# Cosine on one core: whole turns taken off in one VectorE operation, the angle counted in turns

## The chip, the core and the metric

One core of one Trainium2 chip runs the whole program. The metric is the time of one execution on the device in microseconds (us); lower is better. The engines are named as in the profile: PE (TensorE), DVE (VectorE), ACT (ScalarE), POOL (GpSimd), SP (SyncE, which here issues most DMAs).

## What is computed

Attention with pooled queries, then a mixture of experts with eight experts of 288 tokens each, then a dense layer pair with a cosine between its halves. The change touches the last function alone:

```python
def _moe_ref(x, w_gate, w1, w2):            # x: 2304 x 512, 8 experts, 288 tokens each
    ...
    for e in range(E):
        mask = assigned == e
        h = np.maximum(x[mask] @ w1[e], 0.0)
        out[mask] = h @ w2[e]

def _moe2_ref(x, w_in, w_out):              # 2304 x 512, 512 x 2048, 2048 x 512
    h = x @ w_in
    g = h * np.cos(h)
    return g @ w_out
```

The inputs are 64-bit or 32-bit floats of which the kernel makes a high and a low float16 half each; a product of two such matrices is three float16 matmuls (high with high, high with low, low with high).

## The kernel before, in words

**Stages.** The attention takes the first 450 us or so of the span. Then comes `moe`: the tokens are routed to the eight experts one expert after the other (`route`), and each expert's rows run through three passes in the order of the table `PLAN`: `ffn1(i)` for expert i (two matmuls with a ReLU between them, L1353 and L1367), `ffn2_in(j)` for block j of 256 tokens (the product with `w_in`, L1429, and the cosine), and `ffn2_out(j)` (the product with `w_out`, L1454). From expert 2 on, PLAN is `ffn1(j)`, `ffn2_in(j)`, `ffn2_out(j)` for j = 2, 3, ... , and block 8 comes last without an `ffn1`.

**The cosine.** `ffn2_in(j)` fills eight banks of PSUM per block, one for each pair of feature tiles: 24 matmuls of 256 columns a bank (2 tiles, 4 slices of the contraction, 3 products). For each bank `cosine` runs a chain over 128x512 elements. `u` is the bank (the trace calls it `h`), scaled by the constant `U_UP`. ACT writes the number of whole turns as an integer (L1396, T for short below). DVE takes `turns` times 2 pi off in two steps, with the high part of 2 pi (L1398) and with its low part (L1400). ACT takes the sine of half the angle (L1402) and squares it (L1404). DVE forms the product with `u` (L1407), which frees the bank. ACT rounds it to float16 (L1412, `gh`), and POOL subtracts that from it (L1414, `gl`). L1398 and L1407 read one operand from PSUM and one from SBUF; L1400 reads both from SBUF. The tile `turns` has four buffers (`TB`), `r1` has three, and there are four banks.

**Who else is at work then.** The search of `route` is a chain of rounds (8 for an expert): DVE compares (L999, `ge`), PE counts (L965 for the first three experts, L976 and L985 for the later ones, with a copy L981 or, on ACT, L979 between the two), DVE compares with the room left (L1009, `hit`), PE sums (L1012), and DVE makes the next candidates (L1014 `near`, L1023, L1027 `cand`). Weights of the next expert land by DMA (L1249 and L1251, on SP's queue), ACT rounds them (L1278) and DVE makes the low halves (L1282). Up to about 590 us the 64-bit `w_out` is decoded as well (`split64`: L228, L241 to L256, on SP, DVE, ACT and POOL). The tokens of the next expert are gathered by POOL (L1205) and transposed by DMA (L1214, SP).

**What sets the order.** Each engine runs its instructions in the order in which they were written, and a class `Order` decides that order while the program is built: each task says with `yield ENGINE, size` what it wants next, and `Order.go` gives each engine to the request that could start first by a table of costs (`COST`: a fixed part, a part per element and a latency, for DVE 0.07 us, 0.00105 us and 0.15 us). A request that is taken away or made shorter therefore moves the instructions of all engines from there on. An engine does not pass over an instruction that waits.

Of the kernel before, what the change touches and what calls it, by code (L numbers as in the profile page):

```python
# [13 lines left out]
AF = mybir.ActivationFunctionType  # L14
OP = mybir.AluOpType
# [28 lines left out]
PE, ACT, DVE, POOL, SP = "PE", "ACT", "DVE", "POOL", "SP"  # L44
# [23 lines left out]
U_UP = Y_UP * WIN_UP  # L68
O_EVAC = -2.0 / (U_UP * WOUT_UP)
TWO_PI = 2.0 * math.pi  # L70
PI_HI = round(TWO_PI * 512.0) / 512.0
PI_LO = TWO_PI - PI_HI

class Order:
# [31 lines left out]
    def start(self, task, rank, at=None):  # L108
        t = self.now
        if at is not None:  # L110
            self.now = at
        self.resume(task, rank)
        self.now = t

    def mark(self, *key, at=None):

        t = self.now
        self.done[key] = t if at is None else at
        for since, rank, task in self.parked.pop(key, []):
            self.now = max(self.done[key], since)  # L120
            self.resume(task, rank)
        self.now = t
# [795 lines left out]
def moe(od, tc, logits, x_dram, list_dram, before, same, ones, fixed, wih, wil, todo, w1, w2, w_out, out):  # L918
    nc = tc.nc
    V = nc.vector  # L920
    with ExitStack() as ctx:
# [375 lines left out]
        def y_tile(j):  # L1297
            if j not in yT:
                yT[j] = tuple(ac.tile([128, KD, NB], F16, name=n, bufs=3) for n in ("yh", "yl"))
            return yT[j]  # L1300
# [10 lines left out]
        def bank():  # L1311

            b = next(banks)
            if b >= 4:
                yield "read", b - 4
            return b, ps.tile([128, 512], F32, name="h", bufs=4)
# [56 lines left out]
        def g_tiles():  # L1373
            return [ac.tile([128, NF2, NB], F16, name=n) for n in ("gh", "gl")]
# [3 lines left out]
        def ffn2_in(j):  # L1378
            yh, yl = y_tile(j)
            gh, gl = halves[j] = g_tiles()  # L1380
            who = range(j * NB // CAP, ((j + 1) * NB - 1) // CAP + 1)
            for i in who:
                yield "listed", i
            nc.sync.dma_start(rows_sb[:, 2 * j:2 * j + 2], list_dram[j * NB:(j + 1) * NB, 0].rearrange("(c p) -> p c", p=128))

            def cosine(u, f, b):

                n = NF2 // 2 * j + f // 2
                if n >= TB:
                    yield "cosine", n - TB  # L1390
                if n >= TB - 1:
                    yield "product", n - TB + 1
                yield ACT, 512
                turns = ac.tile([128, 512], I32, name="turns", bufs=TB)
                r = ac.tile([128, 512], F32, name="r1", bufs=TB - 1)
                nc.scalar.activation(turns, u, AF.Copy, scale=1.0 / (TWO_PI * U_UP))  # L1396
                yield DVE, 512
                V.scalar_tensor_tensor(r, turns, -PI_HI * U_UP, u, op0=OP.mult, op1=OP.add)  # L1398
                yield DVE, 512
                V.scalar_tensor_tensor(r, turns, -PI_LO * U_UP, r, op0=OP.mult, op1=OP.add)  # L1400
                yield ACT, 512
                nc.scalar.activation(r, r, AF.Sin, scale=0.5 / U_UP)  # L1402
                yield ACT, 512
                nc.scalar.activation(r, r, AF.Square)  # L1404
                yield DVE, 512
                g = turns.bitcast(F32)
                V.scalar_tensor_tensor(g, r, 0.5, u, op0=OP.subtract, op1=OP.mult)  # L1407
                mark("read", b)
                mark("product", n)
                yield ACT, 512  # L1410
                g = g.rearrange("p (e n) -> p e n", e=2)
                nc.scalar.activation(gh[:, f:f + 2], g, AF.Copy)  # L1412
                yield POOL, 512
                nc.gpsimd.tensor_tensor(gl[:, f:f + 2], g, gh[:, f:f + 2], op=OP.subtract)  # L1414
                mark("g", j, f)
                mark("cosine", n)


            for f in range(0, NF2, 2):
                b, u = yield from bank()  # L1420
                for e in range(2):
                    fs = slice((f + e) * 128, (f + e + 1) * 128)
                    for kk in range(KD):
                        for i in who:
                            yield "y", i, kk
                        yield "win", kk * (F2 // NW) + (f + e) * 128 // NW
                        yield PE, 3 * NB
                        for z, (x, y) in enumerate(((wih, yh), (wih, yl), (wil, yh))):
                            nc.tensor.matmul(u[:, e * NB:(e + 1) * NB], x[:, kk, fs], y[:, kk],  # L1429
                                             start=kk == 0 and z == 0, stop=kk == KD - 1 and z == 2)  # L1430
                start(cosine(u, f, b), 1)
# [64 lines left out]
```

## Time and profile before

| what | us |
| --- | --- |
| median of 3 runs | 1140.61 |
| lowest and highest | 1136.2 and 1143.11 |
| the profiled execution, its own time | 1142.8 |
| its span in the profile | 1140.8 |
| PE busy in the span | 1033.8 (91%) |
| DVE, ACT, POOL busy | 825.4, 706.0, 575.3 |

The span runs from the first to the last recorded instruction; 2.0 us of the profiled execution lie around it. "Busy" is the union of an engine's instructions. A matmul's end is modelled and lies behind the start of the next one, so that a busy PE can still be waited on for a little. In brackets behind an instruction of the timeline stand the idle time in front of it and the instruction that ended it. The granted clock is TensorE's, as a share of full speed (2.4 GHz), so that 0.50 is the lower of its two levels, 1.2 GHz.

### The profile page before, as it was taken

Reading aid. Unit: us, or ns where it says so; the run is one execution under the profiler, and the core shown is the slowest. Engines: PE = TensorE matmul, PEld = TensorE weight load, DVE = VectorE, ACT = ScalarE, POOL = GpSimd, SP = SyncE. Lnnn points to the kernel's source line nnn. Section 1 sums busy time; section 2 is a strip of 40 time slices with the busy share of each in tenths; the row PEclk is TensorE's granted clock in tenths of the full one; section 3 lists DMA queues with packets and bytes.
Section 4 is the critical chain, followed back from the end, with each engine's and each line's share of the span. In section 5 each row is a group of like instructions: output and inputs, shape, how many; then the busy total and the mean of one; then the engine's idle time right before and its main releaser. Section 6 shows DMA issues by size and latency. Waiting matters only on the chain. (4 is left out here: it accounts for less than half of the span.)

```text
span 1140.8 us, 25414 instructions
## 1 busy us (share of the span) xinstructions
PE 1033.8 (91%) x10020; PEld 714.7 (63%) x10020; DVE 825.4 (72%) x1816; ACT 706.0 (62%) x1314; POOL 575.3 (50%) x591
## 2 busy tenths in 40 slices
PE   4898999989998998339889999999999999999997
PEld 2465666656665666227755758577585775858673
DVE  7988988889988887688987818749387482732642
ACT  3888989899998996346863526437154362632542
POOL 4789989888999897442651221313203132130312
PEclk7999999999999999559989999999999999999999
DMA  8987878867765641475616213231331350300000
GB/s 206 233 169 157 178 164 171 171 159 169 158 143 135 132 96 39 143 161 164 183 63 175 84 40 96 76 100 35 114 96 57 106 143 19 95 10 10 4 17 18
DMA packets 187383, 128.00 MB, mean 112 GB/s; under 512 B 138944, under 2 KB 157376, under 8 KB 187264
## 3 DMA queue, kind: packets, MB, share of 16 engines
q1 hardware_dynamic: 184000, 116.36, 42.7%
q0 software_dynamic: 2976, 9.44, 2.5%
q8 instruction: 78, 1.28, 0.5%
q10 hardware_dynamic: 288, 0.59, 0.2%
q14 instruction: 41, 0.34, 0.1%
HBM read 83.40 MB, written 9.45 MB: 81 GB/s over the span
## 5 line engine op out<-in xcount | busy, mean ns | idle before, releaser
L673 POOL TENSOR_TENSOR pl<-p,ph 128x512 f16<-128x512 f32 x192 | 239.2, 1260 | 31.8 <-ACT ph L668 24.4
L1414 POOL TENSOR_TENSOR gl<-turns,gh 128x512 f16<-128x512 f32 x72 | 96.0, 1338 | 282.5 <-ACT gh L1412 281.8
L568 DVE TENSOR_REDUCE nm<-s 128x1 f32<-128x512 f32 x288 | 185.1, 678 | 13.8 <-PE s L526 13.0
L1429 PE MATMUL h<-yl,wih 128*128 128x256 f16 x576 | 157.7, 274 | 2.5 <-DVE yl L1339 2.5
L1429 PE MATMUL h<-yh,wih 128*128 128x256 f16 x576 | 157.8, 274 | 1.8 <-DVE turns L1407 1.8
L1429 PE MATMUL h<-yh,wil 128*128 128x256 f16 x576 | 157.7, 274 | 0.0
L687 PE MATMUL t<-q,k 128*128 128x512 f16 (+1 forms) x576 | 136.0, 291 | 11.0 <-ACT p L664 7.0
L526 PE MATMUL s<-k,q 128*128 128x512 f16 (+3 forms) x480 | 126.3, 341 | 21.2 <-DVE nm L568 15.2
L688 PE MATMUL t<-q,k 96*128 96x512 f16 (+1 forms) x576 | 136.5, 291 | 0.6 <-DMA q<-q 0.6
L664 ACT ACTIVATE p<-t 128x512 f32<-128x512 f32 (+1 forms) x208 | 115.0, 581 | 18.8 <-PE t L688 14.0
L708 PE MATMUL acc<-vv,ph 128*128 128x130 f16 (+1 forms) x1124 | 119.2, 222 | 0.0
L1429 PEld LDWEIGHTS <-wih 128*128 128x128 f16 x1152 | 108.4, 98 | 17.1 <-DVE turns L1407 2.3
L708 PE MATMUL acc<-vv,pl 128*128 128x65 f16 (+1 forms) x1124 | 112.6, 192 | 0.0
L1454 PE MATMUL o<-woh,gl 128*128 128x512 f16 x288 | 109.2, 379 | 2.7 <-POOL gl L1414 2.6
L708 PEld LDWEIGHTS <-ph 128*128 128x128 f16 (+1 forms) x1152 | 101.8, 106 | 15.2 <-issue 7.5
L668 ACT ACTIVATE ph<-p 128x512 f16<-128x512 f32 x180 | 111.1, 642 | 0.4
L1327 DVE SCALAR_TENSOR_TENSOR hl<-h,hh 128x288 f16<-128x288 f32 x64 | 29.1, 455 | 111.4 <-ACT hh L1325 95.1
L1454 PE MATMUL o<-woh,gh 128*128 128x512 f16 x288 | 109.1, 379 | 0.0
L1454 PE MATMUL o<-wol,gh 128*128 128x512 f16 x288 | 109.1, 379 | 0.0
L708 PEld LDWEIGHTS <-pl 128*128 128x128 f16 (+1 forms) x1152 | 93.7, 102 | 11.4 <-POOL pl L673 1.0
L1353 PE MATMUL h<-xx,w1h 128*128 128x288 f16 x512 | 99.9, 296 | 0.0
L1454 PEld LDWEIGHTS <-gh 128*128 128x128 f16 x576 | 53.3, 98 | 59.5 <-issue 2.5
(226 smaller groups left out, 2469.5 us busy)
## 6 DMA issues: line engine op xcount, KB each, us to landing
wraw<-in_moe_w_dram SPq DMA_DIRECT2D x64, 512.0 KB, 4.7
vr<-in_v_dram SPq DMA_DIRECT2D x32, 288.0 KB, 3.7
kr<-in_k_dram SPq DMA_DIRECT2D x30, 288.0 KB, 3.3
qr<-in_q_dram SPq DMA_DIRECT2D x32, 256.0 KB, 3.1
raw<-in_moe_w_in_dram SPq DMA_DIRECT2D x16, 512.0 KB, 5.1
raw<-in_moe_w_out_dram SPq DMA_DIRECT2D x16, 512.0 KB, 4.0
k<-k SPq DMA_DIRECT2D x32, 144.0 KB, 3.6
x_dram<-xs SPq DMA_DIRECT2D x16, 160.0 KB, 2.5
```

Of the source, the lines that this page charges most:

```text
L526: T.matmul(to[lo:hi], ops["q", u][0][:, c, lo:hi], ops["k", u, i][0][:, keys, :].rearrange("p a b -> p (a b)"), start=True, stop=True)
L568: V.tensor_reduce(st["nm", u][:, c, g:g + 1], s, AX.X, OP.max)
L664: A.activation(f[:, :w], s[:, :w], AF.Exp, scale=QK_DOWN)
L668: A.activation(ph[:, b], f[:, :w], AF.Copy)
L673: G.tensor_tensor(pl[:, b], f[:, :w], ph[:, b], op=OP.subtract)
L687: T.matmul(s[:, to:to + w], k1[:, j], q1[:, cols], start=True, stop=False)
L688: T.matmul(s[:, to:to + w], k2[0:96, j], q2[0:96, cols], start=False, stop=True)
L708: T.matmul(acc[lo:hi, to + a:to + 2 * (D + 1)], t[z][:, at:at + hi - lo], vv[:, j, a:], start=j == first and z == 0 and to == 0, stop=j == ...
L1353: nc.tensor.matmul(ph[:, :CAP].rearrange("p (j t) -> p j t", j=3), x[:, kk, fs], y[:, :, kk], start=kk == 0 and z == 0, stop=kk == KD - 1 ...
L1414: nc.gpsimd.tensor_tensor(gl[:, f:f + 2], g, gh[:, f:f + 2], op=OP.subtract)
L1429: nc.tensor.matmul(u[:, e * NB:(e + 1) * NB], x[:, kk, fs], y[:, kk], start=kk == 0 and z == 0, stop=kk == KD - 1 and z == 2)
L1454: nc.tensor.matmul(po, x[:, f, cs], y[:, f], start=f == 0 and z == 0, stop=f == NF2 - 1 and z == 2)
```

## The change

DVE's two operations on `turns` become one. It multiplies `u` by the same factor with which ACT counted the turns, and subtracts the integer from it: what is left is the angle in turns, between -0.5 and 0.5, and the sine takes it times pi. The new operation reads its first operand from PSUM and its second (integers) from SBUF. The constants of 2 pi's two parts go.

```diff
-PI_HI = round(TWO_PI * 512.0) / 512.0
-PI_LO = TWO_PI - PI_HI
...
                 nc.scalar.activation(turns, u, AF.Copy, scale=1.0 / (TWO_PI * U_UP))
                 yield DVE, 512
-                V.scalar_tensor_tensor(r, turns, -PI_HI * U_UP, u, op0=OP.mult, op1=OP.add)
-                yield DVE, 512
-                V.scalar_tensor_tensor(r, turns, -PI_LO * U_UP, r, op0=OP.mult, op1=OP.add)
+                V.scalar_tensor_tensor(r, u, 1.0 / (TWO_PI * U_UP), turns, op0=OP.mult, op1=OP.subtract)
                 yield ACT, 512
-                nc.scalar.activation(r, r, AF.Sin, scale=0.5 / U_UP)
+                nc.scalar.activation(r, r, AF.Sin, scale=math.pi)
```

Lines of the changed kernel behind the cosine have numbers lower by 3 than before (L1407 is L1404 there), lines of `moe` ahead of it by 2 (L999 is L997, L1282 is L1280), and the new operation is L1397.

One request for DVE fewer per bank moves the order of every engine from the first cosine on; nothing stands differently ahead of it. On DVE in `ffn2_in(0)`, in the later rounds of a search, there stood before (`mag` is a step of decoding `w_out`, `w1l` and `w2l` are low halves of expert weights, `r` the cosine's angle, a number behind a name tells buffers apart):

```order
L999 TENSOR_TENSOR ge<-near,cand 128x270
L1398 SCALAR_TENSOR_TENSOR r_10185<-turns,h 128x512
L241 SCALAR_TENSOR_TENSOR mag<-raw_10017,near 128x512
L1009 TENSOR_SCALAR hit_10229<-r,room 8x15
L1400 SCALAR_TENSOR_TENSOR r_10185<-turns,r_10185 128x512
L1014 SCALAR_TENSOR_TENSOR near<-r,wbit 128x15
L1407 SCALAR_TENSOR_TENSOR turns<-r_10127,h 128x512
L1023 TENSOR_REDUCE near<-near 128x1
L1282 SCALAR_TENSOR_TENSOR w1l<-wraw,w1h 128x512
L1027 TENSOR_TENSOR cand<-near,kbit 128x15
L1282 SCALAR_TENSOR_TENSOR w2l<-wraw,w2h 128x512
L999 TENSOR_TENSOR ge<-near,cand 128x270
```

Now a round that belongs to the same pass reads:

```order
L250 TENSOR_TENSOR low<-low,sg 128x512
L1404 SCALAR_TENSOR_TENSOR turns<-r_10072,h 128x512
L1007 TENSOR_SCALAR hit_10159<-r,room 8x15
L1397 SCALAR_TENSOR_TENSOR r_10124<-h,turns 128x512
L1012 SCALAR_TENSOR_TENSOR near<-r,wbit 128x15
L1021 TENSOR_REDUCE near<-near 128x1
L1025 TENSOR_TENSOR cand<-near,kbit 128x15
L997 TENSOR_TENSOR ge<-near,cand 128x270
```

Of six operations of 512 elements in a round three are left here. The first four rounds of that pass hold as many as before, because weights and decoding (`w1l`, `w2l`, `mag`, `low`, `wol`) have moved up into them.

On DVE in `ffn2_in(2)`, a round of a later search, before:

```order
L1009 TENSOR_SCALAR hit_12135<-r,room 128x15
L1398 SCALAR_TENSOR_TENSOR r_12125<-turns,h 128x512
L1014 SCALAR_TENSOR_TENSOR near<-r,wbit 128x15
L1400 SCALAR_TENSOR_TENSOR r_12125<-turns,r_12125 128x512
L1023 TENSOR_REDUCE near<-near 128x1
L1407 SCALAR_TENSOR_TENSOR turns<-r_12074,h 128x512
L1027 TENSOR_TENSOR cand<-near,kbit 128x15
L999 TENSOR_TENSOR ge<-near,cand 128x270
L1398 SCALAR_TENSOR_TENSOR r_12168<-turns,h 128x512
L981 CAST part<-r 90x48
```

And a round now:

```order
L1007 TENSOR_SCALAR hit_12087<-r,room 128x15
L1404 SCALAR_TENSOR_TENSOR turns<-r_12030,h 128x512
L1012 SCALAR_TENSOR_TENSOR near<-r,wbit 128x15
L1021 TENSOR_REDUCE near<-near 128x1
L1025 TENSOR_TENSOR cand<-near,kbit 128x15
L997 TENSOR_TENSOR ge<-near,cand 128x270
L1404 SCALAR_TENSOR_TENSOR turns<-r_12062,h 128x512
L979 CAST part<-r 90x48
```

From `hit` to the next `part` four operations of 512 elements have become two. On PE the last two counts of such a search now stand 15 matmuls behind the sum before them, all within `ffn2_in`, where before 24 and 15 lay between, the latter within `ffn2_out`.

## Rows read from the trace of the kernel before

**Rows 1.** The page's head and its part 1: busy time of each engine.

```profile
span 1140.8 us, 25414 instructions
...
PE 1033.8 (91%) x10020; PEld 714.7 (63%) x10020; DVE 825.4 (72%) x1816; ACT 706.0 (62%) x1314; POOL 575.3 (50%) x591
```

**Rows 2.** Stretches of 10 us: length, PE, PEld, DVE, ACT, POOL busy (instructions), clock, DMA, GB/s.

```profile
560.00:570.00 10.00, 10.00 (x116) 8.13 (x113) 10.00 (x23) 9.27 (x18) 8.06 (x6) 1.00 0.65 166
570.00:580.00 10.00, 5.87 (x66) 4.05 (x65) 10.00 (x22) 9.54 (x17) 9.68 (x7) 0.77 0.32 92
580.00:590.00 10.00, 10.00 (x73) 6.52 (x72) 7.90 (x19) 6.62 (x12) 6.49 (x5) 0.72 0.04 16
...
720.00:730.00 10.00, 8.36 (x60) 4.30 (x61) 8.36 (x20) 6.00 (x11) 4.24 (x4) 1.00 0.00 0
...
1050.00:1060.00 10.00, 10.00 (x94) 8.96 (x92) 5.68 (x9) 6.17 (x12) 1.16 (x1) 1.00 0.01 2
```

**Rows 3.** Timeline of PE: start, duration, instruction, idle before it and its releaser.

```profile
573.73 0.60 PE L965 MATMUL r<-ge,own 128*8 128x15 f16 x18 [0.95 <-DVE ge L999]
...
579.14 0.60 PE L965 MATMUL r<-ge,own 128*8 128x15 f16 x18 [1.85 <-DVE ge L999]
...
720.54 0.31 PE L976 MATMUL r<-own,ge 128*90 128x48 f16 x3 [0.72 <-DVE ge L999]
...
723.50 0.17 PE L1012 MATMUL r<-hit,ones 128*128 128x15 f16 x1 [0.54 <-DVE hit L1009]
...
727.44 0.31 PE L976 MATMUL r<-own,ge 128*90 128x48 f16 x3 [0.52 <-DVE ge L999]
...
927.29 0.28 PE L1429 MATMUL h<-yh,wih 128*128 128x256 f16 x1 [1.81 <-DVE turns L1407]
...
948.30 0.39 PE L1454 MATMUL o<-woh,gl 128*128 128x512 f16 x1 [0.48 <-POOL gl L1414]
...
1078.17 0.39 PE L1454 MATMUL o<-woh,gl 128*128 128x512 f16 x1 [0.59 <-POOL gl L1414]
...
1080.13 0.39 PE L1454 MATMUL o<-woh,gl 128*128 128x512 f16 x1 [0.48 <-POOL gl L1414]
```

**Rows 4.** One line's instructions: duration in ns (least/median/most), first and last start.

```profile
L1400 DVE SCALAR_TENSOR_TENSOR r<-turns,r x72: 665/815/2419, 550.9 to 1117.2; 128x512 f32<-128x512 int32 x72
...
L1398 DVE SCALAR_TENSOR_TENSOR r<-turns,h x72: 665/680/689, 549.2 to 1116.5; 128x512 f32<-128x512 int32 x72
...
L1327 DVE SCALAR_TENSOR_TENSOR hl<-h,hh x64: 434/457/458, 513.9 to 1037.1; 128x288 f16<-128x288 f32 x64
```

**Rows 5.** Groups by line from 600 us on: count, busy us, mean ns, idle before.

```profile
L1400 DVE SCALAR_TENSOR_TENSOR r<-turns,r 128x512 f32<-128x512 int32 x64 | 70.7, 1104 | 0.8
```

**Rows 6.** Timeline of DVE in `ffn2_in(7)`.

```profile
1052.49 0.69 DVE L1400 SCALAR_TENSOR_TENSOR r<-turns,r 128x512 f32<-128x512 int32 x1
...
1054.99 0.68 DVE L1407 SCALAR_TENSOR_TENSOR turns<-r,h 128x512 f32<-128x512 f32 x1
1055.59 0.68 DVE L1400 SCALAR_TENSOR_TENSOR r<-turns,r 128x512 f32<-128x512 int32 x1
...
1065.20 0.68 DVE L1407 SCALAR_TENSOR_TENSOR turns<-r,h 128x512 f32<-128x512 f32 x1
...
1067.18 1.54 DVE L1400 SCALAR_TENSOR_TENSOR r<-turns,r 128x512 f32<-128x512 int32 x1
1068.65 0.68 DVE L1407 SCALAR_TENSOR_TENSOR turns<-r,h 128x512 f32<-128x512 f32 x1
```

**Rows 7.** Timeline of ACT in `ffn2_in(7)`.

```profile
1053.21 0.63 ACT L1402 ACTIVATE r<-r 128x512 f32<-128x512 f32 x1 [1.48 <-DVE r L1400]
...
1054.25 0.62 ACT L1404 ACTIVATE r<-r 128x512 f32<-128x512 f32 x1
```

**Rows 8.** Timeline of POOL in `ffn2_in(7)`.

```profile
1067.02 1.16 POOL L1414 TENSOR_TENSOR gl<-turns,gh 128x512 f16<-128x512 f32 x1 [2.29 <-ACT gh L1412]
```

**Rows 9.** Timeline of ACT at the start of `ffn2_in(5)`.

```profile
923.06 1.06 ACT L1278 ACTIVATE w2h<-wraw 128x1024 f16<-128x1024 f32 x1 [4.30 <-DMA wraw<-in_moe_w_dram]
```

## Prediction

> **What bounds the kernel now.** I read the page's head first: PE is busy 91% of the span [rows 1], so it is the engine that sets the end, and what DVE saves counts only where PE waits for it. The stretches of 10 us then show how little that is: in most of the second half PE is busy 10.00 of 10.00, as at 1050 us. The holes are at 570 to 590 us, with PE at 5.87 of 10 and the granted clock at 0.77 and 0.72, and at 720 us with 8.36 [rows 2]; the stretches at 790 and 860 us look like that at 720. So I went to PE's timeline and looked at who ends each idle time: behind 550 us it is nearly always DVE or the cosine's chain [rows 3]. Last I asked why DVE is late. The removed operation has a median of 815 ns and reaches 2419, while L1398, which does the same arithmetic with one operand in PSUM, never leaves 665 to 689 ns [rows 4]. The timeline shows why: an L1400 of 1.54 us begins at 1067.18 while POOL's `gl` runs from 1067.02 to 1068.18, and goes through only behind it [rows 6, 8]. Both of L1400's operands lie in SBUF.
>
> **The change part by part.** *What goes from DVE.* 72 operations; 64 of them took 70.7 us, 1104 ns each [rows 5], so about 79 us of DVE in all. What stays is one operation with a PSUM operand, 680 ns like L1398 [rows 4]. ACT, POOL and PE keep all their work. None of the 79 us is on the path as such, for PE covers it; what is on the path are PE's waits, which I take one by one. A matmul of 256 columns is shown with 0.28 us [rows 3] though 94 of them fit into 10 us [rows 2], 0.106 us each, so an idle time in front of one means some 0.17 us more of lost pace. I add that to each wait (for the 512-column matmul as an estimate by the same difference).
>
> *The cosine alone, blocks 7 and 8.* Here DVE has nothing else. From one L1407 to the next it takes 1068.65 - 1065.20 = 3.45 us [rows 6], while PE fills a bank in 24 x 0.106 = 2.55. Five of the eight banks run at that pace, and `ffn2_out` waits twice for `gl`, 0.59 and 0.48 [rows 3], 1.4 us with the pace; block 8 shows the same pair. Without L1400 the cycle in the new order is: DVE's angle to the sine 0.72 (1052.49 to 1053.21), the sine 0.63, the square to the product 0.74 (1054.25 to 1054.99), the product to DVE's next operation 0.60 (1054.99 to 1055.59) [rows 6, 7], 2.69 us in all. Five banks at 0.76 less are 3.8 us, more than the 1.4 waited for. Both blocks: 2.8 us. Bounds 0 and 2.8; the upper one, because nothing else is late next.
>
> *Block 5.* `ffn2_in(5)` waits 1.81 us for a bank [rows 3], 2.0 with the pace. Its cause is a weight for which ACT waits 4.30 us [rows 9], and that stays. Behind it the chain to the first L1407 loses one DVE operation (0.6) and, in the new order, the `turns` of the next bank that stood ahead of the sine on ACT (0.5): 1.1 us, bounds 0 and 2.0. Its `gl` wait of 0.48 [rows 3], 0.65 with the pace, goes as in block 7.
>
> *Blocks 2 to 4, the search.* PE waits 0.72, 0.54 and 0.52 us for `ge` and `hit` at the end of `ffn2_in(2)` [rows 3], 2.3 us with the pace; blocks 3 and 4 repeat it, 6.8 us together. These rounds are queued on DVE behind L1400s that POOL holds. Four large operations between two counts become two, but the order now also puts the last counts only 15 matmuls (1.6 us) behind the sum before them, and a part of the copies sits on ACT. I keep 0.9 us of wait per block and take 4.1; bounds 0 and 6.8.
>
> *Block 0, 560 to 590 us.* DVE is busy 10.00 of 10.00 twice over, and PE waits 0.95 and 1.85 us for `ge` [rows 2, 3] and twice more, shorter, for `hit`. PE's idle time from 570 to 580 is 4.1 us. Then the granted clock falls to 0.77 and 0.72: a mean of full and half rate, so 4.6 and 5.6 us at 1.2 GHz, which cost about 1.4 (PE was busy 0.59 of it) and 2.8 us. Together 8.3 us, the upper bound. The lower is 0, for ACT is busy 9.27 and 9.54 there [rows 2], and DVE stands in line for its squares. In the new order the first four rounds keep their six large operations, since decoding and weights move up; the last three, where PE waited, have about three. I take half, 4.1 us.
>
> *Sum.* 2.8 + 1.1 + 0.65 + 4.1 + 4.1 = 12.75 us, from 1142.8 (the profiled execution) to 1130.0. That execution lies 2.2 us above the median of the runs, so for a median I say 1128.
>
> One rule is weighed here. The rows say that operations with an operand in PSUM are not held by POOL, but none of L1398, L1407 and the new one is alike: the new one reads PSUM first and SBUF second. The nearest row of that operand order is L1327, 434 to 458 ns while POOL was at work beside it [rows 4], so not held. The Trainium skill (SBUF — State Buffer, Who interferes with whom) says that a VectorE instruction with two SBUF inputs brings the second one through an interface shared with GpSimd, and that one with at most one SBUF input, outside the two-port modes, does not contend. Read by its first half alone, the new operation's SBUF input, being the second, would be held, which is rival C; read whole, it is free. The trace agrees with the whole rule for L1398 and L1400, and that lowers C's chance; with the rule or without it the sum is the same.
>
> **The rivals.** *A: ACT and the search's own chain are next.* In block 0 ACT is nearly full, and in blocks 2 to 4 the tighter order eats the gain. Then 2.8 + 1.1 + 0.65 and some 1.5 from the rest remain, 6 us: 1134.6 by the median. For it: ACT's 9.27 and 9.54 [rows 2]. Against: DVE had no idle time there, so ACT was not what it waited for.
>
> *B: every wait named goes.* 2.8 + 2.0 + 0.65 + 6.8 + 8.3 = 20.6 us: 1120. For it: all of them end at DVE or at the cosine [rows 3]. Against: the planner fills what is freed.
>
> *C: the new operation is held like L1400.* Then it takes 1.54 us where POOL runs, the cycle is 2.69 + 0.86 = 3.55, no better than 3.45, and the order counts on time that isn't there: 1141, no gain. Against it L1327 [rows 4].
>
> *D, slower: ACT stands behind weights that land later.* In three blocks the new order issues the weight pieces behind all three transposes of SP's queue, where one went ahead of them before. Should ACT wait for the last piece as in block 5, 4.30 us [rows 9], PE loses 2.0 us a block; if the clock falls after it as at 570 us, 4.2 more. Three blocks: 18.6 us, less the 8.65 that is left of the sum without those blocks' 4.1: 10 us slower, 1150.6. It decides as soon as the last piece lands behind the first sine of its block. Against it: block 1 has that order already and no such wait.
>
> **How the numbers follow.** The forecast has 0.50, A 0.28, B 0.12, C 0.05, D 0.05. The range leaves out D, C and about half of B: 1119 to 1138. A measurement of this kernel tells about 1% from no change, 11.4 us, so the line is at 1129.2. Of the forecast's own spread (8 to 17 us) six tenths lie beyond it: 0.30; with B 0.42, and a little of A's upper end, 0.45 for faster. D gives 0.05 for slower, and 0.50 is left for within 1%.
>
> **What would show it.** Right: L1397 with 665 to 690 ns at all 72; `gl` waits on PE gone in blocks 5, 7 and 8, with about 2.7 us from product to product; PE idle from 570 to 580 us about halved; less than 1.2 us of waits for `ge` and `hit` at the end of blocks 2 to 4. Wrong: an L1397 of over 1 us; a granted clock that falls as before near 575 us (then block 0 gave nothing) or anew elsewhere; waits of ACT for weights in blocks 2 to 4; or waits for `ge` that merely stand at other places.

## The result, and the profile after

The changed kernel took 1123.43 us (median of 4 runs, 1122.43 to 1126.6), the kernel before beside it 1139.03 us (4 runs): a ratio of 0.9865, 95% interval [0.9826, 0.9904]. A second measurement with more runs gave 0.9845 [0.9822, 0.9869] (1123.58 against 1141.82 us, below). So the change is worth 1.3 to 1.6% by the two ratios, and 1.0 to 1.8% by the ends of the two intervals. I had forecast 1128 us; the time lies inside the range.

The page's head and its busy times after, to be set beside [rows 1]:

```profile
span 1124.7 us, 25354 instructions
...
PE 1027.5 (91%) x10020; PEld 714.9 (64%) x10020; DVE 758.8 (67%) x1746; ACT 710.5 (63%) x1317; POOL 554.2 (49%) x586
```

DVE lost 66.6 us of work, and the span 16.1 us. POOL, whose operations the change does not touch, lost 21.1 us as well. The share of PE stayed at 91%: it bounds this kernel as before.

The stretches of [rows 2] after (same columns):

```profile
560.00:570.00 10.00, 8.39 (x87) 6.30 (x85) 9.93 (x21) 6.30 (x12) 3.92 (x3) 0.83 0.58 125
570.00:580.00 10.00, 10.00 (x112) 7.79 (x111) 9.05 (x26) 9.62 (x20) 4.73 (x5) 1.00 0.28 62
580.00:590.00 10.00, 10.00 (x120) 7.27 (x118) 9.14 (x27) 8.87 (x17) 5.67 (x4) 1.00 0.11 41
590.00:600.00 10.00, 7.77 (x62) 5.46 (x60) 9.72 (x31) 3.48 (x8) 1.74 (x1) 1.00 0.60 199
720.00:730.00 10.00, 10.00 (x70) 4.54 (x69) 6.88 (x28) 3.11 (x6) 2.42 (x3) 1.00 0.47 150
1050.00:1060.00 10.00, 10.00 (x76) 7.22 (x74) 4.38 (x8) 8.24 (x15) 4.63 (x4) 1.00 0.00 0
```

The hole from 570 to 590 us is filled and the clock there is full; the hole at 720 us is filled. Two others are there now: 560 to 570 us, with the granted clock at 0.83, and 590 to 600 us, where the kernel before had 8.85 with a wait of its own (1.15 us for `ge` at 591.87).

These are all idle times of PE with a releaser from 560 us to the end, in its timeline. From 600 us on one is left, of 0.20 us; the kernel before had 17 there, 10.5 us together:

```profile
562.81 0.60 PE L963 MATMUL r<-ge,own 128*8 128x15 f16 x18 [1.61 <-DVE ge L997]
...
595.44 0.30 PE L1365 MATMUL h<-hh,w2l 128*128 128x288 f16 x1 [1.87 <-DVE w2l L1280]
...
596.73 0.30 PE L1365 MATMUL h<-hh,w2l 128*128 128x288 f16 x1 [0.33 <-DVE w2l L1280]
...
905.05 0.61 PE L1139 MATMUL r<-ids,oh 128*32 128x9 f16 x18 [0.20 <-DVE oh L1134]
```

Nothing of [rows 3] is left: no wait for `gl`, for `hit` or for the bank in block 5. The new operation, all 72 of it (answers to L1400 in [rows 4]):

```profile
L1397 DVE SCALAR_TENSOR_TENSOR r<-h,turns x72: 668/683/692, 551.7 to 1099.1; 128x512 f32<-128x512 f32 x72
```

It reads PSUM first and SBUF second, and was never held: 26 of the 72 ran beside a POOL operation that reads SBUF, and none took more than 692 ns. L1400 before, counted the same way in the timelines: 22 of 72 ran with no POOL operation beside them, in 665 to 693 ns; of the 48 that ran beside `gl`, 36 took 937 to 2419 ns. The group of POOL's subtraction from 600 us on, before and then after (count, busy us, mean ns):

```profile
L1414 POOL TENSOR_TENSOR gl<-turns,gh 128x512 f16<-128x512 f32 x64 | 83.1, 1304 | 280.0 <-ACT gh L1412 279.2 <-DMA rows<-list_dram 0.7
```

```profile
L1411 POOL TENSOR_TENSOR gl<-turns,gh 128x512 f16<-128x512 f32 x64 | 74.0, 1162 | 270.1 <-ACT gh L1409 263.0 <-issue 5.2 <-DMA list_dram<-r 1.8
```

The hold had worked in both directions: POOL stood behind DVE too (12 of those 48 took 670 to 693 ns), and `gl` is 142 ns an operation shorter without L1400. Which of the two is held depends on which begins first; the rows of e9 in the account of the prediction show that.

The cosine in block 7, on DVE (answers to [rows 6]):

```profile
1043.34 0.69 DVE L1404 SCALAR_TENSOR_TENSOR turns<-r,h 128x512 f32<-128x512 f32 x1 [1.41 <-POOL gl L1411]
1043.94 0.68 DVE L1397 SCALAR_TENSOR_TENSOR r<-h,turns 128x512 f32<-128x512 f32 x1
1046.04 0.69 DVE L1404 SCALAR_TENSOR_TENSOR turns<-r,h 128x512 f32<-128x512 f32 x1 [1.42 <-ACT r L1401]
1046.64 0.68 DVE L1397 SCALAR_TENSOR_TENSOR r<-h,turns 128x512 f32<-128x512 f32 x1
1048.74 0.69 DVE L1404 SCALAR_TENSOR_TENSOR turns<-r,h 128x512 f32<-128x512 f32 x1 [1.41 <-ACT r L1401]
```

From product to product 2.70 us (1043.34, 1046.04, 1048.74), where it was 3.45; DVE now idles 1.4 us in each bank.

Where the time came from is best read per pass. The table gives the time from the first matmul of a pass to that of the next one, in the timelines of PE (us):

| Pass | before | after | gain |
|---|---|---|---|
| block 0: `ffn2_in(0)` and both halves of `ffn1(1)` | 66.94 | 63.29 | 3.65 |
| `ffn2_out(0)`, block 1 | 66.83 | 66.47 | 0.36 |
| blocks 2, 3, 4: `ffn2_in` | 23.58, 23.59, 23.82 | 22.70, 22.69, 22.70 | 2.90 |
| blocks 2, 3, 4: `ffn2_out` | 24.20, 24.21, 24.20 | 22.26, 22.26, 22.25 | 5.84 |
| block 5: in, out | 23.98, 21.62 | 21.87, 20.72 | 3.01 |
| block 6: in, out | 20.96, 20.72 | 20.96, 20.72 | 0 |
| blocks 7 and 8: out | 22.15, 21.94 | 20.72, 20.50 | 2.87 |

Blocks 2 to 4 are to be read as in and out together: in the new order a count of the search stands in `ffn2_in` that stood in `ffn2_out` before. The sum is 18.6 us. The profiled executions differ by 16.2 us (1142.8 and 1126.6), because the first `ffn2_in` began 2.5 us later in the profile after (543.22 against 540.70), ahead of the first cosine; in the second profile of the changed kernel it began at 541.61.

### The profile page after: what moved, and what is told of

The parts are those of the page before. It is cut to its first block, busy times and chain, and to the rows that moved or that the text cites. A ratio compares the mean times of both kernels' runs of the same rounds, so it can differ in the third digit from the quotient of the medians.

```text
span 1124.7 us, 25354 instructions
## 1 busy us (share of the span) xinstructions
PE 1027.5 (91%) x10020; PEld 714.9 (64%) x10020; DVE 758.8 (67%) x1746; ACT 710.5 (63%) x1317; POOL 554.2 (49%) x586
## 5 line engine op out<-in xcount | busy, mean ns | idle before, releaser
L671 POOL TENSOR_TENSOR pl<-p,ph 128x512 f16<-128x512 f32 x192 | 236.4, 1245 | 33.8 <-ACT ph L666 24.2
L1411 POOL TENSOR_TENSOR gl<-turns,gh 128x512 f16<-128x512 f32 x72 | 83.6, 1166 | 281.0 <-ACT gh L1409 273.7
L1433 ACT ACTIVATE ot<-o 128x512 f32<-128x512 f32 x18 | 10.7, 596 | 138.9 <-PE o L1451 138.9
L1351 PE MATMUL h<-xx,w1h 128*128 128x288 f16 x512 | 96.9, 290 | 0.0
```

Source lines behind the costliest of these rows:

```text
L671: G.tensor_tensor(pl[:, b], f[:, :w], ph[:, b], op=OP.subtract)
L1351: nc.tensor.matmul(ph[:, :CAP].rearrange("p (j t) -> p j t", j=3), x[:, kk, fs], y[:, :, kk], start=kk == 0 and z == 0, stop=kk == KD - 1 ...
```

## The experiments

Three explanations fit that table. The hold: the second operation cost because POOL held it. The length: it cost because it stood in the cosine's line on DVE, held or not. The order: the planner's new order of all the other work brought the gain. Five kernels (e1, e2, e3, e5, e6) set these against each other, by the operation (as it was, free of the hold, gone) and by the order (old, new). The others ask about block 0.

**e1: the operation gone, the order of before.** The changed kernel with a request of the old size put back, and no instruction behind it:

```
     V.scalar_tensor_tensor(r, u, 1.0 / (TWO_PI * U_UP), turns, op0=OP.mult, op1=OP.subtract)
+    yield DVE, 512
```

> The one new operation in the order of before (the planner is still asked for two; only the second instruction is missing). Theory O, that the removed operation's own time on DVE made PE's waits: the waits of blocks 2 to 4, 5, 7 and 8 go as in the changed kernel, about 15 us, and block 0 gains some of its 8, so 1119 to 1127 us against 1139. Theory P, that the new order made the gain: no more than 3 us, 1136 us or above.

Measured: 1128.94 us (4 runs, 1127.26 to 1130.98), ratio 0.9873 [0.9843, 0.9904]. All waits of PE from 600 us on:

```profile
PE o L1452 <- POOL gl L1412: 1.1, 2, 0.6
PE r L1139 <- DVE oh L1134: 0.2, 1, 0.2
```

The old order, without the operation, gives the gain. The new order adds nothing beyond the spread of the measurements; in the profiles it takes away the two waits for `gl` above, in block 5 (`ffn2_out(5)` takes 22.30 us here and 20.72 in the changed kernel).

**e2: both operations, the new order.** The kernel before with one request for both:

```
     V.scalar_tensor_tensor(r, turns, -PI_HI * U_UP, u, op0=OP.mult, op1=OP.add)
-    yield DVE, 512
     V.scalar_tensor_tensor(r, turns, -PI_LO * U_UP, r, op0=OP.mult, op1=OP.add)
```

> Both old operations, in the order of the changed kernel (the planner is asked for one, and the second instruction follows the first at once). Theory O: the waits come back, and the order counts on time that is not there, so 1137 to 1145 us. Theory P: 1123 to 1128 us.

Measured: 1165.82 us (4 runs, 1162.9 to 1172.71), ratio 1.0216 [1.0173, 1.0259]: slower than before, with the same instructions, and further than either theory had it. Its longest waits of PE from 540 us on (us in total, times, longest):

```profile
PE r L1012 <- DVE hit L1009: 7.8, 13, 1.4
PE r L976 <- DVE ge L999: 6.1, 7, 1.3
PE r L965 <- DVE ge L999: 4.4, 4, 2.6
```

And three sines on ACT in `ffn2_in(2)`:

```profile
728.01 0.63 ACT L1401 ACTIVATE r<-r 128x512 f32<-128x512 f32 x1 [1.81 <-DVE r L1399]
...
731.45 0.63 ACT L1401 ACTIVATE r<-r 128x512 f32<-128x512 f32 x1 [0.58 <-DVE r L1399]
...
734.89 0.63 ACT L1401 ACTIVATE r<-r 128x512 f32<-128x512 f32 x1 [0.69 <-DVE r L1399]
```

From sine to sine 3.44 us, 0.74 more than the 2.70 of block 7 in the changed kernel: about one DVE operation. In the new order the cosine's line is serial, one bank after the other, and an operation more in it counts in full. `ffn2_in(2)` takes 28.95 us in place of 22.70; e5 below tells length from hold in it.

**e3: the operation free of the hold, the old order.** The kernel before; the second operation reads the bank in PSUM in place of `r`, and so repeats the first. Count, requests and order stay as before:

```
-    V.scalar_tensor_tensor(r, turns, -PI_LO * U_UP, r, op0=OP.mult, op1=OP.add)
+    V.scalar_tensor_tensor(r, turns, -PI_HI * U_UP, u, op0=OP.mult, op1=OP.add)
```

> The order and the number of operations of before, but the second operation reads one operand from PSUM (it repeats the first one, so the low part of 2 pi is left out of the angle and its product). Theory H, that POOL's hold made the waits: the second operation takes 0.68 us throughout, the waits of blocks 2 to 4 go, 1125 to 1130 us. Theory L, that one more operation in the line is enough: blocks 7 and 8 keep a cycle near 3.3 us and most of their waits, the searches keep theirs, 1134 to 1139 us.

Measured: 1128.95 us (4 runs, 1126.69 to 1130.37), ratio 0.9869 [0.9839, 0.99]. The line, and then DVE in block 7:

```profile
L1400 DVE SCALAR_TENSOR_TENSOR r<-turns,h x72: 664/678/689, 553.5 to 1102.0; 128x512 f32<-128x512 int32 x72
```

```profile
1046.47 0.69 DVE L1398 SCALAR_TENSOR_TENSOR r<-turns,h 128x512 f32<-128x512 int32 x1 [0.68 <-ACT turns L1396]
1047.19 0.69 DVE L1400 SCALAR_TENSOR_TENSOR r<-turns,h 128x512 f32<-128x512 int32 x1
1047.80 0.68 DVE L1407 SCALAR_TENSOR_TENSOR turns<-r,h 128x512 f32<-128x512 f32 x1
1049.09 0.69 DVE L1398 SCALAR_TENSOR_TENSOR r<-turns,h 128x512 f32<-128x512 int32 x1 [0.61 <-ACT turns L1396]
1049.82 0.69 DVE L1400 SCALAR_TENSOR_TENSOR r<-turns,h 128x512 f32<-128x512 int32 x1
1050.42 0.68 DVE L1407 SCALAR_TENSOR_TENSOR turns<-r,h 128x512 f32<-128x512 f32 x1
```

All 72 operations are still there, and the time is that of the kernel without them. The cycle is 2.62 us (1047.80 to 1050.42), PE's own pace: `ffn2_in(7)` takes 20.96 us for eight banks. The 3.3 us that theory L had did not come, because DVE makes the next bank's angle ahead of the product of the bank before, so two banks are under way and the 0.7 us lie beside ACT's work. In this order the operation's length costs nothing that these measurements show; its hold is the whole price.

**e5: free of the hold, the new order.** e2 with the second operation of e3:

```
     V.scalar_tensor_tensor(r, turns, -PI_HI * U_UP, u, op0=OP.mult, op1=OP.add)
-    yield DVE, 512
-    V.scalar_tensor_tensor(r, turns, -PI_LO * U_UP, r, op0=OP.mult, op1=OP.add)
+    V.scalar_tensor_tensor(r, turns, -PI_HI * U_UP, u, op0=OP.mult, op1=OP.add)
```

> As e2_two_ops_new_order, but the second operation reads one operand from PSUM (it repeats the first, so the low part of 2 pi is left out). Theory H, that POOL's hold is what costs, in the new order too: 1126 to 1134 us. Theory L, that in the new order, where DVE handles one bank after the other, every operation lengthens the line that PE waits for: 1150 us or more, near e2's 1.02 of before.

Measured: 1154.94 us (4 runs, 1152.72 to 1157.41), ratio 1.0102 [1.0078, 1.0126].

```profile
L1399 DVE SCALAR_TENSOR_TENSOR r<-turns,h x72: 686/687/689, 549.9 to 1129.1; 128x512 f32<-128x512 int32 x72
```

Not one operation is held, and the kernel is still slower than before, as theory L had it. `ffn2_in(2)` takes 26.55 us: of the 6.25 us between the changed kernel and e2, 3.85 are length and 2.40 hold. In block 7 the sines follow each other every 3.42 us in e5 and in e2 alike. With e1 to e3 that gives the whole picture (ratios to the kernel before):

| | as it was | free of the hold | gone |
|---|---|---|---|
| old order | 1 | 0.9869 (e3) | 0.9873 (e1) |
| new order | 1.0216 (e2) | 1.0102 (e5) | 0.9865 and 0.9845 (after, twice) |

In the old order the hold is 1.3% and the length nothing beyond the spread. In the new one the hold is 1.1% and the length some 2.5%. The changed kernel gets the same from either order, since it has neither.

**e6: the hold taken from POOL's side.** The kernel before with POOL's subtraction made a write that reads nothing:

```
-    nc.gpsimd.tensor_tensor(gl[:, f:f + 2], g, gh[:, f:f + 2], op=OP.subtract)
+    nc.gpsimd.memset(gl[:, f:f + 2], 0.0)
```

> The kernel before, with POOL's subtraction for gl replaced by a fill of gl with zeros, which reads nothing from SBUF (the low half of the product's left operand is left out). Theory H, by which it is POOL's reading of SBUF that holds an operation with two SBUF operands: L1400 falls to about 0.69 us in blocks 1 to 8 and the time to 1126 to 1131 us (0.985 to 0.990 of before). If any POOL instruction held it, or if the length of DVE's line counted: 1136 us or above, no change.

Measured: 1128.65 us (4 runs, 1125.78 to 1132.92), ratio 0.9875 [0.9844, 0.9906]. DVE's second operation is untouched, and POOL's line is below it:

```profile
L1400 DVE SCALAR_TENSOR_TENSOR r<-turns,r x72: 668/684/1297, 553.1 to 1099.8; 128x512 f32<-128x512 int32 x72
...
L1414 POOL MEMSET gl<- x72: 520/542/552, 559.0 to 1082.6; 128x512 f16 x72
```

The same gain again, and L1400's median falls from 815 to 684 ns with its own operands as they were. POOL's operation is also shorter here (542 against 1158 ns) and seldom at work beside L1400: 61 of the 72 ran with nothing on POOL. So the time alone would not tell reading from length. The instructions that did meet do, though they are few: three L1400s ran beside the fill alone and took 691 or 692 ns, and the one of 1297 ns ran beside L252, a POOL multiplication that reads SBUF. With e3 that gives the pair, DVE's two SBUF operands and POOL's read of SBUF. The Trainium skill (SBUF — State Buffer, Who interferes with whom) says that a VectorE instruction with two SBUF inputs contends with a GpSimd instruction that reads SBUF and not with one that only writes it. The traces agree with it: 36 of 48 L1400s beside `gl` took 937 ns or more before, and in e6 the three beside the fill took 692 ns at most.

**e4: block 0 in the old order, the rest in the new.** The changed kernel with the old request kept in block 0, to be rid of the new waits there:

```
+    if j == 0:
+        yield DVE, 512
```

> The changed kernel, with the planner asked for two operations in block 0 alone. If the new order of block 0 causes the waits that came anew there (1.61 us for a count at 563 us, 1.87 and 0.33 us for low halves of weights at 595 us), they go and ffn2_in(0) to ffn2_out(0) loses 3 to 5 us: 1118 to 1121 us. If they come from ACT and POOL being full there, whatever the order, it stays at 1122 to 1125 us.

Measured: 1128.12 us (4 runs, 1125.71 to 1131.27), ratio 0.9872 [0.9837, 0.9906]. The expected gain did not come. Two stretches of it:

```profile
570.00:580.00 10.00, 7.33 (x94) 5.25 (x93) 9.02 (x20) 9.40 (x18) 7.40 (x7) 0.85 0.31 66
580.00:590.00 10.00, 9.91 (x77) 6.62 (x78) 9.09 (x19) 7.88 (x15) 7.27 (x6) 0.81 0.13 50
```

The new waits went, and the old hole with its lower clock came back at 570 us, smaller than in [rows 2]. Block 0 takes 64.63 us. By its ratio the time is that of the second branch (1124.5 us on the scale of 1139), though the waits went as in the first.

**e7 and e8: the old request in one half of block 0 alone**, on the changed kernel, first e7, then e8:

```
+    if j == 0 and f < 8:
+        yield DVE, 512
```

```
+    if j == 0 and f >= 8:
+        yield DVE, 512
```

> The changed kernel, with the planner asked for two operations in the first four banks of block 0, so that fewer weights and decodings with two SBUF operands are moved up into its first rounds. If those, held by POOL, cause the wait for a count near 563 us: ffn2_in(0) takes 30 to 31 us in place of 32.9; with the weights' low halves still late in ffn1(1) the sum of block 0 is 61 to 63 us against 63.3 and the time 1121 to 1124 us times the drift of before.

> The changed kernel, with the planner asked for two operations in the last four banks of block 0. If the lateness of the weights' low halves comes from the order of those rounds, the 1.87 us wait in ffn1(1) goes and block 0 takes 60 to 62 us against 63.3; if not, no change beyond 1 us.

Measured: e7 1123.64 us, ratio 0.982 [0.9803, 0.9837], block 0 in 61.21 us; e8 1126.55 us, ratio 0.984 [0.9821, 0.986], block 0 in 66.95 us. In e8 the waits for `w2l` went, but block 0 came out 3.66 us longer than in the first profile of the changed kernel, which neither branch had; waits for `ge` (1.82 and 1.21 us), `hit` (0.96) and `hl` (0.63) stand there, and why was not followed up. e7 looked like a version better than the changed kernel, so both were measured side by side.

**e9 and e10: the changed kernel (e9) and e7 (e10) again, side by side, without a new edit.** The expectation of e10 speaks of eight banks; its edit is that of e7, the first four.

> The changed kernel once more, in more rounds and beside the next one on the same chip, to tell whether the next one is better than it. Both theories: a ratio of 0.983 to 0.988 to the kernel before, block 0's three passes 63.3 us, with the 1.6 us wait for ge and the waits for w2l of 1.9 and 0.3 us.

> The changed kernel, with the second request on VectorE kept for the first eight banks of block 0 alone, once more in more rounds. If the 2.1 us that its profile showed in block 0 are a gain of the whole (theory: block 0's passes set the end one for one), it stands 0.0018 below the changed kernel's ratio of the same chip. If the planner's order behind block 0 or the spread of the runs eats it (rival), the two ratios are the same within 0.001.

Measured: e9 (the changed kernel) 0.9845 [0.9822, 0.9869], 1123.58 us (5 runs, 1122.81 to 1127.61); e10 0.9838 [0.9818, 0.9859], 1124.67 us (5 runs, 1123.24 to 1125.63). The difference of 0.0007 is below what these tell apart: e7 is no better version. The profiles say why. Block 0 takes 60.92 us in e9, against 63.29 in the first profile of the very same kernel, and 63.07 us in e10, against 61.21 in e7. Here are the stretch from 560 us and the wait of PE in e9:

```profile
560.00:570.00 10.00, 9.21 (x103) 7.62 (x98) 9.69 (x22) 8.17 (x17) 4.82 (x4) 1.00 0.80 166
```

```profile
565.30 0.60 PE L963 MATMUL r<-ge,own 128*8 128x15 f16 x18 [0.79 <-DVE ge L997]
```

The same instructions in the same order, but the wait for `ge` is 0.79 in place of 1.61 us, stands 23.7 us into the pass in place of 19.6 us (from 541.61 and 543.22), and the clock stays full. It is another count: the one that waited 1.61 us runs at 559.65 without a wait here, and the one that waits here ran at 569.29 without a wait in the first profile. Block 0 thus scatters by some 2.4 us from one execution to the next, and differences of that size between e4, e7 and the changed kernel, read from one profile each, say nothing. Some of it stands ahead of the first cosine: PE's wait for `yl` at the start of `ffn2_in(0)` is 2.49 us in the first profile, 3.44 in e4, 3.15 in e7 and 4.10 in e10. My expectation for e9 of 63.3 us for block 0 missed for the same reason.

## Why the prediction was right, and where it was off

**The mechanism was right.** The step "an L1400 of 1.54 us begins at 1067.18 while POOL's `gl` runs from 1067.02 to 1068.18, and goes through only behind it" carries the change: e3 and e6 each take the hold away, one on DVE's side and one on POOL's, and each gives the ratio of the kernel without the operation. Rival C (the new operation is held as well) fell with 692 ns as the most of 72. The row set against it beforehand was thinner than it read: of the 64 L1327s only five ran beside an arithmetic operation of POOL. Rival D (ACT behind weights) did not appear: PE waits for no bank in blocks 2 to 4. Rival A (ACT and the search's own chain next) fell too.

**The size was too small**: 12.75 us forecast, 16.2 us between the profiled executions, 18.6 us over the passes that the change touches. By terms:

- *Blocks 7 and 8*: 2.8 forecast, 2.87 measured. The cycle was forecast as 2.69 us and is 2.70.
- *Block 5*: 1.1 and 0.65 forecast, 2.11 and 0.90 measured. The 0.90 holds the 0.65 and a wait without a bracket of 0.23, of the kind described next. The step that failed reads: "Its cause is a weight for which ACT waits 4.30 us [rows 9], and that stays." It did not stay; more below.
- *Blocks 2 to 4* are the step that was mis-sized: "I keep 0.9 us of wait per block and take 4.1; bounds 0 and 6.8." Measured 8.74, above my upper bound. Two errors add up. No wait remained, so the 2.7 us that I kept went too; my reason for keeping them, counts that follow the sums too closely, did not bear out. And I took only the waits that carry a bracket in the timeline, while shorter ones carry none. They show when the kernel before is set beside e3, whose PE runs the same instructions in the same order. The three waits of block 2 (0.72, 0.54 and 0.52 us) cost 0.89, 0.70 and 0.68 us there, so 0.16 to 0.17 us of pace each, as forecast. Two more stand without a bracket. PE before:

```profile
716.62 0.27 PE L1429 MATMUL h<-yh,wil 128*128 128x256 f16 x1
717.01 0.17 PE L1012 MATMUL r<-hit,ones 128*128 128x15 f16 x1
...
728.01 0.38 PE L1454 MATMUL o<-woh,gl 128*128 128x512 f16 x1
728.43 0.31 PE L985 MATMUL r<-same,part 90*128 90x15 f16 x6
```

And the first of the two places in e3:

```profile
716.90 0.27 PE L1429 MATMUL h<-yh,wil 128*128 128x256 f16 x1
717.01 0.17 PE L1012 MATMUL r<-hit,ones 128*128 128x15 f16 x1
```

From start to start it is 0.39 and 0.42 us before, and 0.11 and 0.21 in e3: 0.28 and 0.20 us lost. Blocks 3 and 4 repeat both, and block 4 has a third of 0.23. That is 1.7 us in all. With 6.8 for the waits in brackets and 0.04 us behind each `ge` of them, 0.2 us, it makes the 8.7.

- *Block 0*: 4.1 forecast, 3.65 in one profile and 6.02 in the other (66.94 less 60.92). The size is right, the way there only in part. The old waits and the fall of the clock at 570 us went altogether, not by half. New waits took a part back in the first profile, and the clause "waits for `ge` that merely stand at other places" came true here.

On ACT's weight in block 5, these are the roundings of `w2h` in the timeline of ACT, first after, then in e3, which keeps the order of before:

```profile
904.26 2.95 ACT L1276 ACTIVATE w2h<-wraw 128x1024 f16<-128x1024 f32 x3
...
907.99 1.05 ACT L1276 ACTIVATE w2h<-wraw 128x1024 f16<-128x1024 f32 x1
```

```profile
911.67 1.06 ACT L1278 ACTIVATE w2h<-wraw 128x1024 f16<-128x1024 f32 x1 [1.82 <-DMA wraw<-in_moe_w_dram]
```

After, ACT does not wait for the last piece at all; in e3 it waits 1.82 us where [rows 9] has 4.30, and PE does not feel it (`ffn2_in(5)` takes 21.87 us in both). A wait for a transfer was no fixed part of the stage, and I should not have kept it as one. Whether 4.30 us is what the kernel before waits in every execution was not measured.

What fills DVE in block 0 is seen in the profile after. DVE, and then POOL beside it:

```profile
557.00 1.44 DVE L254 TENSOR_TENSOR wol<-low,woh 128x512 f16<-128x512 f32 x1
558.36 1.76 DVE L1280 SCALAR_TENSOR_TENSOR w1l<-wraw,w1h 128x512 f16<-128x512 f32 x1
560.04 0.17 DVE L1012 SCALAR_TENSOR_TENSOR near<-r,wbit 128x15 int32<-128x15 f32 x1
...
562.33 0.43 DVE L997 TENSOR_TENSOR ge<-near,cand 128x270 f16<-128x270 f32 x1
```

```profile
556.73 1.16 POOL L1411 TENSOR_TENSOR gl<-turns,gh 128x512 f16<-128x512 f32 x1 [0.62 <-ACT gh L1409]
557.84 1.72 POOL L246 TENSOR_TENSOR mag<-mag,low 128x512 int32<-128x512 int32 x1
```

The same two DVE operations and the same `gl` in e9, DVE and then POOL:

```profile
555.00 0.67 DVE L254 TENSOR_TENSOR wol<-low,woh 128x512 f16<-128x512 f32 x1
555.60 0.67 DVE L1280 SCALAR_TENSOR_TENSOR w1l<-wraw,w1h 128x512 f16<-128x512 f32 x1
```

```profile
555.09 2.21 POOL L1411 TENSOR_TENSOR gl<-turns,gh 128x512 f16<-128x512 f32 x1 [0.47 <-ACT gh L1409]
```

The decoding and the weights' low halves have two operands in SBUF as well. In the first profile `gl` begins ahead of L254, and DVE is held twice, 1.44 us behind `gl` and 1.76 us while L246 runs to 559.56. In e9 L254 begins 0.09 us ahead of `gl`: DVE's two take 0.67 us each, and `gl` is held for 2.21 us. From L254's start to that of `ge` it is 5.33 us in the first profile and 3.50 in e9 (555.00 to 558.50), and PE's wait for this `ge`, 1.61 us at 562.81, isn't there in e9. So the hold makes this new wait, and which engine begins first decided between these two executions. The planner's `COST` knows nothing of the hold, so what it pulls forward into the freed time can cost more than planned. That the waits for `w2l` come from the hold as well is not shown.

**The chances.** The ratio came out beyond the line of 1%, on the side that I had given the smaller chance: "within 1%" had 0.50 and "faster" 0.45, because I let the forecast's own sum of 12.75 us stand close to the line of 11.4 us and kept waits for which no row spoke. Rival B ("every wait named goes") held for all blocks but block 0: the passes behind block 0 gave 15.0 us (18.62 less 3.65), where B has 12.3 (20.6 less 8.3) and the forecast 8.65. The measured time lies between B's 1120 and the forecast's 1128.

## What to carry to other kernels

An operation's price is what it queues behind: 72 operations of 0.68 us cost nothing where another bank's work covers them, and 1.3% of the kernel where POOL's read of SBUF held them. Moving one operand to PSUM, or letting POOL read nothing, brought as much as removing the operation. Where a planner sets the order, judge an edit's order apart from its work: the same two operations were 2.2% slower under the order that suits one, and taking their hold away as well still left them 1.0% slower than before.

## What the runs showed that I had not expected

- The hold is mutual: POOL's subtraction fell from a mean of 1304 to 1162 ns when L1400 went, without an edit of it. In e9 it took 2.21 us behind a DVE operation that began 0.09 us earlier.
- A wait costs PE more than its idle time by a steady amount: 0.16 to 0.17 us more at each of the three in block 2, beside e3, and 0.36 for the two in `ffn2_out(7)` (0.59 and 0.48 idle, 1.43 gained). A wait too short for a bracket costs it too: 0.28 and 0.20 us in block 2.
- The same kernel, twice profiled, had a granted clock of 0.83 and of 1.00 from 560 to 570 us, behind a wait of 1.61 us and with one of 0.79 us. A part of the program this close to a change of the clock differs by 2.4 us from execution to execution.
